# Batch 0 in two passes over half the weights, with the weight conversion spread over 24 units

## The chip, the cores and the metric

The kernel runs on one core of a Trainium2 chip. The core has five engines with queues of their own: TensorE (PE, its weight loads shown apart as PEld), VectorE (DVE), ScalarE (ACT), GpSimd (POOL) and SyncE (SP), which here only issues DMAs. The metric is the device time of one execution in microseconds (us); the time of a kernel is the median over runs. A profile is one execution more, with every instruction's start and end; its span is the time from the first to the last instruction, and its own device time is a little longer than the span.

## What is computed

The input x has 8 batches of 3008 positions by 256 channels. The reference takes the real part of a two-dimensional Fourier transform of each batch and sends every position through a two-layer network with a soft threshold between the layers:

```
X = np.fft.fft(np.fft.fft(x, axis=1), axis=2).real
h = X @ w_in
g = np.where(h >= 1, h, np.where(h <= -1, 0.0, (h + 1) ** 2 / 4))
out = g @ w_out
```

w_in is 256 by 2048 and w_out 2048 by 256. Both come as 64-bit floats, of which the kernel sees the two 32-bit halves.

## The kernel before

**Units.** A batch is cut into 3 chunks (one of 482 columns, two of 512; each column stands for a position and its mirror image, the two signs `sg`), and the 2048 hidden channels into 16 tiles `f` of 128. One chunk with one `f` is a unit; 8 x 3 x 16 = 384 units in all, taken chunk by chunk, `f` from 0 to 15 in each. `gemm1(i)` (from L343) makes the hidden values of unit i: six matmuls into two PSUM banks of the tag `uv` (three banks), then on DVE `us` (L356) and the two halves of `h` (L358, L359), then on ACT the soft threshold's square `a` (L362, L363), then on DVE the minimum and maximum that join them (`g`, L368 or L372). `gemm2(i)` (from L385) multiplies with w_out and adds into four PSUM banks, one for each half of the output channels and each sign. It runs four units behind `gemm1` (`LAG`), and at the last `f` of a chunk the four sums are copied out (L413 to L417) and sent to DRAM.

**Precision.** PE multiplies in a fast format after a value is split into a high and a low part, three products for each one. In the first 16 units (`NATIVE`) `gemm2` multiplies plain 32-bit floats instead, one slower product each, so that w_out need not be split yet and `g` need not be split at all. From unit 16 on, `gh` (ACT, L375) and `gl` (POOL, L377) are the parts of `g`.

**Weights.** Sixteen jobs of 512 KB convert the weights, eight for each matrix, in the order in, in, out, out for each quarter of the hidden channels. A job's steps have letters: `l` the load (SP), `a` two integer operations on DVE (L185, L186), `b` three ACT operations (L191 to L193), `c` two DVE operations (L198, L199), and the multiplication L212, called `d` where POOL does it and `v` where DVE does. A quarter of w_in is then folded with two small matrices on PE, because the real transform over the channels is moved into the weights (`f`, L231 and L232; two folds for a quarter), and split (`s`, L246). Row 0 of the second fold is brought into a column `delta` by four DMAs issued by ACT (L238). `o` splits an eighth of w_out (L152, L153).

**Transforms.** The Fourier transform of a batch is eight pieces of stage 1 (an addition `y`, matmuls L260, copies `z`), one small piece `nyquist`, whose row goes through DRAM and comes back spread over all partitions (`nyb`), and six pieces of stage 2 (matmuls L320, split into `pqh` and `pql`). For batch 0 the pieces stand in the start's hand-written list `START` and in `STEPS`; for a batch b+1 they lie between the units of batch b.

**Order.** `START` and `STEPS` are lists of such steps. Up to unit 15 (`PINNED`) every engine runs in exactly the order of the program text. Later the framework's scheduler orders by priority. In a unit the steps ahead of the bar `|` run between `a` and `g`, those behind it after `g`. A buffer tag has a few slots; a tile takes a slot when one is free, and a slot is free when all that reads its last tile is done. The tags that matter: `h` and `a` (three slots each, shared by the units' tiles and by the jobs' working tiles, even jobs in `h`, odd ones in `a`), `gh` and `gl` (four), `xt` (four input tiles), `o` (two output tiles).

Of the kernel before, what the change touches and what calls it, by code (L numbers as in the profile page):

```python
# [100 lines left out]
def fft_ffn_kernel(ctx: ExitStack, tc: tile.TileContext, x, cst, w_in, w_out, out):  # L101
# [114 lines left out]
    def split_w_out(q):  # L216
# [5 lines left out]
        split(*(wo[t][:, fs].rearrange("p f e -> p (f e)") for t in ("woh", "wol")), wo32[q // 2][:, q % 2])  # L222

    folds = {}

    def fold_w_in(n):
# [6 lines left out]
        if m == 1:  # L233
            row = sb.tile([1, CH], F32, tag="us", name=f"row_{f4}", bufs=2)
            nc.scalar.activation(row, pt[0:1], AF.Copy)
# [322 lines left out]
```

## Time and profile before

| what | us |
|---|---|
| median of 3 runs (lowest, highest) | 1791.31 (1790.23, 1791.47) |
| the profiled execution, device time | 1789.41 |
| its span | 1787.5 |
| PE busy | 1748.2 |
| DVE busy | 1430.2 |
| ACT busy | 1343.0 |
| POOL busy | 1186.5 |

The share of busy time of PE is 98%, so what can be won lies where PE is not busy or runs at a lowered clock. The page's second part shows these places as slices of the span; each of the 40 slices is 44.7 us long.

### The profile page before, as it was taken

The page shows a single profiled execution, that of the slowest core. Times are in us where ns is not written, and L with a number is a line of the kernel's source. Part 1 is how long each engine was busy: PE and PEld are TensorE (multiplying, and loading weights), DVE is VectorE, ACT ScalarE, POOL GpSimd, SP SyncE. Part 2 cuts the span into 40 slices and gives each one's busy share as a digit, 9 for nine tenths or more (in the row PEclk, how much of TensorE's full clock was granted, in tenths as well). Part 3 has the DMA queues.
Part 4 walks back from the last instruction along what each step waited for, and adds up shares of the span by engine and source line. Part 5 has one row for each costly group of instructions (what it writes and reads, how often), then busy time and mean ns, then how long its engine had stood idle before and what let it go on. Part 6 is the DMA issues. An engine that isn't in the chain of part 4 may idle for free.

```text
span 1787.5 us, 21542 instructions
## 1 busy us (share of the span) xinstructions
PE 1748.2 (98%) x7822; PEld 1408.4 (79%) x7822; DVE 1430.2 (80%) x1733; ACT 1343.0 (75%) x1571; POOL 1186.5 (66%) x829
## 2 busy tenths in 40 slices
PE   7789999999999999999999999999999999999998
PEld 5346888888888788887888888888888888887876
DVE  4887788878887888778878788787888788888886
ACT  4666787787777877778777777778777787777775
POOL 1233876777768766777667876677776766767776
PEclk7799999999999999999999999999999999999999
DMA  8111110110010100101001100011000000000000
GB/s 249 36 53 49 45 51 10 50 50 27 24 42 27 49 18 24 51 27 53 30 1 51 49 30 30 9 51 49 27 24 33 1 23 30 13 24 5 18 24 24
DMA packets 30026, 66.33 MB, mean 37 GB/s; under 512 B 5088, under 2 KB 9312, under 8 KB 29920
## 3 DMA queue, kind: packets, MB, share of 16 engines
q1 hardware_dynamic: 27580, 64.95, 11.2%
q8 instruction: 61, 1.00, 0.2%
q14 instruction: 45, 0.37, 0.1%
q10 hardware_dynamic: 2340, 0.02, 0.1%
HBM read 40.22 MB, written 24.72 MB: 36 GB/s over the span
## 4 chain that ended last, share of the span: by engine, by line
PE 43%; ACT 18%; POOL 16%; DVE 11%; issue 11%; DMA 1%; ACTq 0%; POOLq 0%; SPq 0%; DVEq 0%
PE acc L408 26%; POOL gl L377 15%; PE uv L353 13%; DVE h L372 7%; ACT a L363 6%; ACT gh L375 5%; ACT a L362 4%; PE s L320 2%; PE s L260 1%; ACT z L276 1%; DVE h L358 1%; DVE h L359 1%; POOL y L122 1%; DVE g L368 1%; DVE cv L186 1%
## 5 line engine op out<-in xcount | busy, mean ns | idle before, releaser
L377 POOL TENSOR_TENSOR gl<-h,gh 128x512 fp32r<-128x512 f32 (+1 forms) x736 | 1057.2, 1459 | 448.5 <-ACT gh L375 425.2
L372 DVE SCALAR_TENSOR_TENSOR h<-a,h 128x1024 f32<-128x1024 f32 (+1 forms) x368 | 560.6, 1524 | 236.4 <-ACT a L363 234.8
L375 ACT ACTIVATE gh<-h 128x1024 fp32r<-128x1024 f32 (+1 forms) x368 | 384.6, 1045 | 352.4 <-DVE h L372 338.4
L408 PE MATMUL acc<-gh,woh 128*128 128x512 f32 (+1 forms) x1472 | 586.7, 399 | 3.2 <-DVE o L417 2.2
L408 PE MATMUL acc<-gl,woh 128*128 128x512 f32 (+1 forms) x1472 | 575.3, 391 | 1.0 <-POOL gl L377 0.9
L408 PE MATMUL acc<-gh,wol 128*128 128x512 f32 (+1 forms) x1472 | 575.0, 391 | 0.0
L362 ACT ACTIVATE a<-h,biases 128x1024 f32<-128x1024 f32 (+1 forms) x384 | 431.4, 1124 | 31.3 <-DVE h L359 29.5
L363 ACT ACTIVATE a<-a 128x1024 f32<-128x1024 f32 (+1 forms) x384 | 398.7, 1039 | 7.6
L408 PEld LDWEIGHTS acc<-gh,woh 128*128 128x128 f32 x1472 | 277.7, 189 | 63.9 <-DVE o L417 5.7
L408 PEld LDWEIGHTS acc<-gl,woh 128*128 128x128 f32 x1472 | 277.6, 189 | 62.6 <-POOL gl L377 2.3
L353 PE MATMUL uv<-pqh,wh 128*128 128x512 f32 (+1 forms) x768 | 310.5, 404 | 14.8 <-DVE us L356 8.8
L408 PEld LDWEIGHTS acc<-gh,wol 128*128 128x128 f32 x1472 | 277.3, 188 | 54.4
L358 DVE TENSOR_TENSOR h<-us,uv 128x512 f32<-128x512 f32 (+1 forms) x384 | 259.7, 676 | 67.2 <-POOL gl L377 21.3
L353 PE MATMUL uv<-pql,wh 128*128 128x512 f32 (+1 forms) x768 | 301.6, 393 | 0.0
L353 PE MATMUL uv<-pqh,wl 128*128 128x512 f32 (+1 forms) x768 | 301.3, 392 | 0.0
L356 DVE SCALAR_TENSOR_TENSOR us<-nyb,delta,uv 128x512 f32<-128x512 f32 (+1 forms) x384 | 278.4, 725 | 7.0 <-PE uv L353 6.9
L359 DVE TENSOR_TENSOR h<-us,uv 128x512 f32<-128x512 f32 (+1 forms) x384 | 256.1, 667 | 0.0
L353 PEld LDWEIGHTS uv<-pqh,wh 128*128 128x128 f32 x768 | 145.5, 189 | 60.7 <-DVE us L356 14.6
L353 PEld LDWEIGHTS uv<-pqh,wl 128*128 128x128 f32 x768 | 145.6, 190 | 31.9 <-issue 3.7
L353 PEld LDWEIGHTS uv<-pql,wh 128*128 128x128 f32 x768 | 145.3, 189 | 29.7 <-DVE pql L153 0.2
L122 POOL TENSOR_TENSOR y<-x 96x512 f32<-96x512 f32 x58 | 104.9, 1808 | 31.2 <-PE s L260 16.5
L276 ACT ACTIVATE z<-s 64x192 f32<-64x192 f32 x246 | 83.2, 338 | 21.0 <-PE s L263 9.1
(56 smaller groups left out, 662.1 us busy)
## 6 DMA issues: line engine op xcount, KB each, us to landing
x<-in_x_dram SPq DMA_DIRECT2D x64, 384.0 KB, 3.5
out_dram<-o SPq DMA_DIRECT2D x30, 512.0 KB, 2.8
out_dram<-o SPq DMA_DIRECT2D x16, 482.0 KB, 2.9
nyb<-nyr SPq DMA_DIRECT2D x24, 256.0 KB, 3.3
raw<-in_moe_w_in_dram SPq DMA_DIRECT2D x4, 512.0 KB, 5.4
raw<-in_moe_w_out_dram SPq DMA_DIRECT2D x4, 512.0 KB, 10.6
raw_woh<-in_moe_w_out_dram SPq DMA_DIRECT2D x2, 512.0 KB
raw_woh<-in_moe_w_in_dram SPq DMA_DIRECT2D x2, 512.0 KB, 3.5
```

Source lines behind the costliest of these rows:

```text
L122: (engine or nc.gpsimd).tensor_tensor(y, t[:, 0], t[:, 1], op=ALU.add)
L276: nc.scalar.activation(dst, src, AF.Copy)
L353: nc.tensor.matmul(t[:, :n], w[m][:, cols], r[:, m, :n], start=(j == 0), stop=(j == 2))
L356: nc.vector.scalar_tensor_tensor(us, nyb[b, k][:, :n], delta[:, f : f + 1], uv[0], op0=ALU.mult, op1=ALU.add)
L358: nc.vector.tensor_tensor(h[:, 0], us, uv[1], op=ALU.subtract)
L359: nc.vector.tensor_tensor(h[:, 1], us, uv[1], op=ALU.add)
L362: nc.scalar.activation(a, h, AF.Relu, bias=half, scale=0.5)
L363: nc.scalar.activation(a, a, AF.Square)
L372: nc.vector.scalar_tensor_tensor(h, a, 1.0, h, op0=ALU.min, op1=ALU.max)
L375: nc.scalar.activation(gh, h, AF.Copy)
L377: nc.gpsimd.tensor_tensor(gl[:, sg], h[:, sg], gh[:, sg].bitcast(F32), op=ALU.subtract)
L408: nc.tensor.matmul(acc[:, :n], w, g[:, sg], start=(f == 0 and j == 0), stop=(last and j == len(terms) - 1))
```

## The change

1. **Two passes over batch 0.** The list `units` replaces the division of i by 16. In batch 0 the three chunks are first taken with `f` 0 to 7 (units 0 to 23), then with `f` 8 to 15 (units 24 to 47). At the end of a chunk's first pass its four sums go through `o` tiles to a DRAM tile; two units before the end of its second pass they are loaded again, and the copy at the end becomes an addition on DVE for all four.
2. **14 jobs over 24 units.** Because the second half of the weights is first used in unit 24, `STEPS` now reaches from unit 0 to 23: a full job in each of units 0 to 3, about half a job in each later one. `EARLY_BANKS` goes from 18 to 13, `PINNED` from 16 to 18, and the pieces of batch 1 start at unit 18 (`NEXT`) instead of 16.
3. **`d` becomes `v`.** All 14 multiplications L212 of these jobs move from POOL to DVE. Their buffers change: the last two of w_out stay in the job's working tile.
4. **g one unit later.** Up to unit 18, `activate(i - 1)` runs after the `h` of unit i.
5. **delta by matmuls.** Four matmuls of one row each and one ACT copy replace four DMAs issued by ACT.
6. **The start.** All additions `y` on DVE, two of them ahead of the first fold, the loads l4 and l5 ahead of the rest, the `nyquist` piece's copies ahead of the others, nine warm-up matmuls instead of seven and in one bank.
7. **Smaller moves.** The folding matrices use a slot of `nyb`; for later batches `nyquist_spread` is issued at the start of each pair of stage 2 pieces instead of three at once.

```diff
 START = (
-    "l0 k l1 m0 x0 x1 x2 x3 x4 x5 x6 x7 "
-    "a0 b0 a1 b1 c0 v0 y0 p0 z0 p8 c1 v1 y1 p1 z1 Y2 f0 y3 s0 p2 z2 Y4 f1 y5 s1 p3 p4 w3 y6 w4 p5 w5 y7 p6 w6 p7 w7 "
-    "l4 n0 l5 l2 l3 l8 l9 l6 l7 l12 l13 n1 l10 l11 n2 l14 l15 p9 q9 p10 q10 a4 b4"
+    "l0 k l1 m0 x0 x1 x2 x3 x4 x5 x6 x7 l4 l5 "
+    "a0 b0 a1 b1 c0 v0 y0 p0 t0 z0 c1 y1 v1 p1 p8 z1 n0 l2 l3 l6 l7 n1 l8 l9 l10 l11 n2 l12 l13 l14 l15 "
+    "y2 y3 f0 p2 z2 p3 s0 y4 w3 f1 y5 p4 p5 y6 s1 w4 e0 p6 w5 y7 p7 w6 w7 p9 p10 q9 q10 a4 b4"
 )
 STEPS = {
-    0: "c4 d4 a5 b5 |",
-    1: "c5 d5 a2 b2 |",
-    2: "f2 f3 c2 d2 a3 b3 | s2 s3",
-    3: "p11 c3 d3 a8 b8 | q11",
...
-    17: "o7 |",
+    0: "c4 v4 a5 b5",
+    1: "c5 v5 a2 b2",
+    2: "f2 f3 c2 v2 a3 b3 s2 s3",
+    3: "e1 c3 v3 a6 b6",
+    4: "c6 v6 p11 q11",
+    5: "a7 b7",
+    6: "c7 v7 p12 q12",
+    7: "a8 b8",
+    8: "c8 v8",
+    9: "a9 b9",
+    10: "c9 v9 a10 b10",
+    11: "f4 f5 s4 s5",
+    12: "e2 c10 v10 p13 q13",
+    13: "a11 b11",
+    14: "c11 v11 p14 q14",
+    15: "o0 o1 a12 b12",
+    16: "c12 v12 o2",
+    17: "o3 a13 b13",
+    18: "c13 v13 o4",
+    19: "o5 a14 b14",
+    20: "f6 f7 s6 s7",
+    21: "e3 c14 v14 a15 b15",
+    22: "o6 c15 v15",
+    23: "o7",
 }
-RAW = {0: "gh", 1: "gh", 4: "gh", 5: "gh", 2: "woh", 3: "woh", 8: "woh", 9: "woh"}
-RAW |= {6: "wol", 7: "wol", 12: "wol", 13: "wol", 10: "xt", 11: "xt", 14: "xt", 15: "xt"}
+RAW = {0: "gh", 1: "gh", 4: "gh", 5: "gh", 2: "woh", 3: "woh", 6: "woh", 7: "woh"}
+RAW |= {8: "wol", 9: "wol", 10: "wol", 11: "wol", 12: "xt", 13: "xt", 14: "xt", 15: "xt"}
...
+    def spread_delta(f4):
+        row = deltas.pop(f4)
+        pt = fft_bank(0, f"delta_{f4}")
+        for i in range(4):
+            nc.tensor.matmul(pt[:, i : i + 1], row[:, i * P : (i + 1) * P], one[0:1], start=True, stop=True)
+        nc.scalar.activation(delta[:, f4 * 4 : f4 * 4 + 4], pt[:, :4], AF.Copy)
...
-            with nc.allow_non_contiguous_dma(reason="one row of w_in to a column"):
-                for i in range(4):
-                    nc.scalar.dma_start(
-                        delta[:, f4 * 4 + i : f4 * 4 + i + 1], row[:, i * P : (i + 1) * P].rearrange("o (p x) -> o p x", x=1)
-                    )
+            deltas[f4] = row
...
+    units = [(0, k, f) for v in range(2) for k in range(NCHUNK) for f in range(v * NFT // 2, (v + 1) * NFT // 2)]
+    units += [(b, k, f) for b in range(1, NB) for k in range(NCHUNK) for f in range(NFT)]
...
+    def load_parts(k):
+        for dh in range(2):
+            o = outs[k, dh] = sb.tile([P, 2, CH], F32, tag="o", name=f"os_{k}_{dh}", bufs=2)
+            nc.sync.dma_start(o[:, :, : WIDTH[k]], parts.pop((k, dh))[:, :, : WIDTH[k]])
...
+                        if add:
+                            nc.vector.tensor_tensor(o[:, sg, :n], acc[:, :n], o[:, sg, :n], op=ALU.add)
+                        elif sg:
...
+            if half_way:
+                parts[k, dh] = dr.tile([P, 2, CH], F32, tag="part", name=f"part_{k}_{dh}", bufs=6)
+                nc.sync.dma_start(parts[k, dh][:, :, :n], o[:, :, :n])
...
-            gemm1(i, STEPS.get(i, ""))
+            gemm1(i)
+            if b == 0 and r > per // 2 and r % (NFT // 2) == NFT // 2 - 2:
+                load_parts(units[i][1])
+            if i <= PINNED and i:
+                activate(i - 1)
+            if i >= PINNED:
+                activate(i)
+            run_steps(STEPS.get(i, ""))
```

More of the change, by code (lines that the diff above doesn't have):

```diff
@@ L136, in fft_ffn_kernel @@
     delta = wts.tile([P, NFT], F32, name="delta")
-    biases = wts.tile([P, 3], F32, name="biases")
-    for i, v in enumerate((0.5, 1151.0, 255.0 * 2**23)):
+    biases = wts.tile([P, 4], F32, name="biases")
+    for i, v in enumerate((0.5, 1151.0, 255.0 * 2**23, 1.0)):
         nc.vector.memset(biases[:, i : i + 1], v)
-    half, above, top = (biases[:, i : i + 1] for i in range(3))
+    half, above, top, one = (biases[:, i : i + 1] for i in range(4))
     early = [0]
@@ L221, in split_w_out @@
         fs = slice(q * m, (q + 1) * m)
-        split(*(wo[t][:, fs].rearrange("p f e -> p (f e)") for t in ("woh", "wol")), wo32[q // 2][:, q % 2])
-    folds = {}
+        split(*(wo[t][:, fs].rearrange("p f e -> p (f e)") for t in ("woh", "wol")), wo32[q])
+    folds, deltas = {}, {}
+    def spread_delta(f4):
[4 more added lines that the diff above has]
+        nc.scalar.activation(delta[:, f4 * 4 : f4 * 4 + 4], pt[:, :4], AF.Copy)
     def fold_w_in(n):
@@ L264, in stage1_sums, with stage1_last @@
         s1[b, q] = bank
+    def stage1_last(b, bank):
+        pd = bank[:NA, GPC * 96 : GPC * 96 + 2 * NC]
+        for m in range(2):
+            nc.scalar.activation(zt[b][m * NA : (m + 1) * NA, :, P], pd[:, m * NC : (m + 1) * NC], AF.Copy)
     def stage1_copy(b, q, vector=False):
         z, bank = zt[b], s1.pop((b, q))
+        if q == 0 and b:
+            stage1_last(b, bank)
         pt = bank[:, : GPC * 96].rearrange("p (i n) -> p i n", i=GPC)
@@ L312, in stage2_sums @@
         if h % 2 == 0:
+            if b:
+                nyquist_spread(b, k)
             pq[b, k] = tuple(
@@ L339, in fft_pieces, with gemm1 @@
         return pieces
-    acts = {}
-    def gemm1(i, steps):
-        bk, f = divmod(i, NFT)
-        b, k = divmod(bk, NCHUNK)
+    units = [(0, k, f) for v in range(2) for k in range(NCHUNK) for f in range(v * NFT // 2, (v + 1) * NFT // 2)]
+    units += [(b, k, f) for b in range(1, NB) for k in range(NCHUNK) for f in range(NFT)]
+    n_units = len(units)
+    per = NCHUNK * NFT
+    fronts, acts = {}, {}
+    def gemm1(i):
+        b, k, f = units[i]
         n = WIDTH[k]
@@ L363, in gemm1, with activate @@
         nc.scalar.activation(a, a, AF.Square)
-        before, after = steps.split("|") if steps else ("", "")
-        run_steps(before)
+        fronts[i] = h, a
+    def activate(i):
+        n = WIDTH[units[i][1]]
+        h, a = fronts.pop(i)
         if i < NATIVE:
@@ L369, in gemm1 @@
             acts[i] = (g,)
-            run_steps(after)
             return
@@ L408, in gemm2 @@
                     nc.tensor.matmul(
-                        acc[:, :n], w, g[:, sg], start=(f == 0 and j == 0), stop=(last and j == len(terms) - 1)
+                        acc[:, :n], w, g[:, sg], start=(begin and j == 0), stop=(last and j == len(terms) - 1)
                     )
@@ L424, in fft_ffn_kernel @@
     nc.gpsimd.memset(warm, 0.0)
-    for _ in range(7):
-        nc.tensor.matmul(fft_bank(0, "warm"), warm[:, :P], warm, start=True, stop=True)
+    warm_bank = fft_bank(0, "warm")
+    for _ in range(9):
+        nc.tensor.matmul(warm_bank, warm[:, :P], warm, start=True, stop=True)
     n1 = XC
```

67 lines of the change are left out of this document (25 added, 42 removed).

## The prediction

> **What bounds the kernel now.** First the busy time in four stretches (columns: stretch, its length, then busy us and count for PE, PEld, DVE, ACT, POOL, then PE's granted clock, the DMA share, GB/s).
>
> ```profile
> 39.70:63.00 23.30, 17.59 (x41) 10.30 (x41) 22.20 (x33) 14.84 (x20) 5.07 (x5) 0.65 0.41 141
> 63.00:150.00 87.00, 74.30 (x214) 40.60 (x213) 72.79 (x101) 53.42 (x72) 22.00 (x19) 0.91 0.12 32
> 150.00:188.30 38.30, 38.30 (x159) 27.25 (x158) 30.64 (x38) 30.23 (x44) 21.70 (x16) 1.00 0.19 59
> 188.30:1787.50 1599.20, 1590.17 (x7307) 1311.43 (x7305) 1289.46 (x1531) 1228.49 (x1400) 1132.64 (x780) 1.00 0.09 30
> ```
>
> After 150 us PE is full, so only the first 150 us can get shorter, or the rest get worse. Between 40 and 63 us DVE is busy 22.2 of 23.3, with PE at 0.65 of its clock. Next, PE's prices, from the chain that ended last (start, length, what).
>
> ```profile
> 140.00 4.68 PE acc L408 x8
> 144.68 1.31 PE uv L353 x6
> 145.99 3.23 PE acc L408 x8
> ...
> 169.94 1.40 PE uv L353 x6
> 171.33 0.87 PE s L260 x8
> 172.20 2.82 PE acc L408 x12
> ...
> 188.49 1.39 PE uv L353 x6
> ```
>
> A gemm1 costs 1.31 at 482 columns and 1.39 at 512; a gemm2 of plain floats 3.23 at 482, so 3.43 at 512; a split one 2.82; a transform piece about 0.9. At 172.20 stands the first split product, gemm2 of unit 16, behind gemm1 of unit 20; four gemm1 on, **gemm1 of unit 24 starts at 188.49**. That is my marker: the changed kernel has by then laid out all weights too, and from there both have the same full PE. Now DVE's prices between 40 and 150 us (groups by shape: count, busy us, mean ns, idle before), and one group, L358, from 300 to 1700 us.
>
> ```profile
> L368 DVE SCALAR_TENSOR_TENSOR g<-a,h 128x964 f32<-128x964 f32 x15 | 17.7, 1180 | 4.4 <-issue 2.6 <-ACT row L235 1.1 <-ACT a L363 0.7
> ...
> L356 DVE SCALAR_TENSOR_TENSOR us<-nyb,delta,uv 128x482 f32<-128x482 f32 x15 | 10.6, 707 | 0.3 <-PE uv L353 0.3
> ...
> L186 DVE TENSOR_SCALAR cv<-raw_woh 128x512 uint32<-128x512 uint32 x4 | 6.1, 1513 | 0.0
> ```
> ```profile
> L358 DVE TENSOR_TENSOR h<-us,uv 128x512 f32<-128x512 f32 (+1 forms) x319 | 215.6, 676 | 55.2 <-POOL gl L377 18.7 <-DVE us L356 1.0 <-PE uv L353 0.5
> ```
>
> A unit needs 0.71 + 2 x 0.68 + 1.18 = 3.2, and about 3.0 at 482 columns, as neighbours on DVE overlap by 0.08 (at 68.35 below, 0.69 ends past 68.96); 3.2 at 512. With a whole job on top DVE is the bound: PE needs only 1.31 + 3.23 = 4.5 a unit. L186 is the odd one:
>
> ```profile
> 40.62 0.42 DVE L186 TENSOR_SCALAR cv<-raw 128x512 uint32<-128x512 uint32 x1
> 45.03 1.38 POOL L212 TENSOR_TENSOR cv<-cv 128x512 f32<-128x512 f32 x1 [18.75 <-DVE cv L199]
> 127.64 1.29 POOL L122 TENSOR_TENSOR y<-x 96x512 f32<-96x512 f32 x1 [1.49 <-DMA x<-in_x_dram]
> 128.04 1.44 DVE L198 SCALAR_TENSOR_TENSOR cv<-raw,cv 128x512 f32<-128x512 uint32 x1
> ```
>
> Alone it takes 0.42; where POOL's multiplication L212 runs beside it, 1.5 (the group's mean; in each unit with a job POOL starts one like that of 45.03). DVE waits for POOL there; at 128.04 L198 takes 1.44 instead of 0.69, beside one of POOL's additions.
>
> **The change, part by part. The start.** Rows of the timeline:
>
> ```profile
> 11.44 0.31 SPq L115 DMA_DIRECT2D x<-in_x_dram  x1
> 13.50 0.69 DVE L212 TENSOR_TENSOR cv<-cv 128x512 f32<-128x512 f32 x1
> 21.51 1.91 PE L231 MATMUL wps<-cv,cm 128*128 128x512 f32 x4
> 24.55 2.62 ACTq L238 DMA_DIRECT2D delta<-row  x4
> 27.22 2.09 ACT L276 ACTIVATE z<-s 64x192 f32<-64x192 f32 x6 [2.70 <-issue]
> 35.27 3.75 PE L320 MATMUL s<-cs,z 128*128 128x128 f32 x16 [1.63 <-DVE z L274]
> 41.32 0.72 DVE L356 SCALAR_TENSOR_TENSOR us<-nyb,delta,uv 128x482 f32<-128x482 f32 x1 [0.27 <-PE uv L353]
> 68.35 0.69 DVE L153 TENSOR_TENSOR pql<-s,pqh 128x512 fp32r<-128x512 f32 x1 [0.96 <-ACT pqh L152]
> 68.96 0.71 DVE L356 SCALAR_TENSOR_TENSOR us<-nyb,delta,uv 128x482 f32<-128x482 f32 x1
> ```
>
> Four delta DMAs hold ACT for 2.6 us just ahead of the copies that stage 2 (35.27) waits for. They go; in their place four tiny matmuls, which the trace doesn't show, cost PE between nothing and 1.7, twice the stage 1 piece of eight records (0.87 at the full clock); I take 0.9, that piece. The input additions go earlier and the first fold no longer stands ahead of two of them, for which I take another 2.3. Stage 2 then starts 4.9 sooner, at 30.4, and `us` of unit 0 at 36.4 instead of 41.3. Ends: 2.6 (only the DMAs) and 8.7, where the last input sets it: its load is issued at 11.44, and the start's loads take 11 us to land (11.2 by the next row), so about 22.7 plus an addition, a piece and its copies.
>
> ```profile
> DMA to landing us min/median/max: 10.9/11.2/12.3
> ```
>
> **Units 0 to 3.** Before, `us` of unit 4 starts at 68.96, 27.6 behind that of unit 0. Four L186 fall from 1.51 to 0.42: -4.4. Four multiplications come from POOL: 4 x 0.69 = +2.8. The first g leaves unit 0: -1.1. The stage 2 split at 68.35 moves to unit 4 with its wait of 0.96: -1.6. New is a wait: g late means `h` of unit 1 still holds its slot when unit 2 asks for one; the other two hold jobs 4 and 2. Job 4's is freed by folds f2 and f3 on PE, and `us` of unit 2 is queued ahead on DVE. At the clock of 0.65 a fold takes 1.91 / 0.65 = 2.9; f3 can't start before `us` of unit 2, so `h` waits about 3.0, and behind it on DVE g, c2, v2, a3. Sum 26.3; `us` of unit 4 at 62.7.
>
> That clock is a choice. With the clock restored the wait is 2.0 and all is 1 us earlier. The row for it:
>
> ```profile
> 136.72 0.77 PE L353 MATMUL uv<-pqh,wh 128*128 128x482 f32 x1 [3.60 <-DVE us L356]
> ```
>
> After this gap of 3.60 the next gemm2 takes 4.68 (at 140.00 above), the one behind it 3.23. The Trainium skill, "TensorE: Matmul & The Clock Gate", What's actually happening, has PE fall to half its clock after an idle window of about 3.4 us and rise again after one of busy work. That speaks against this part of the change, which leaves PE 1.3 us of work in units of 5; the trace agrees (4.68). By the rule the folds would run at half clock, f3 would take 3.8, and the sum would be 1 us later than mine.
>
> **Units 4 to 10** carry half a job each: c and v 1.8 (three operations of 0.69, less the overlaps), or a 0.7 (twice 0.42), and unit 4 and 6 a split of 0.6. DVE: 5.4 + 3.7 + 5.4 + 3.7 at 482 columns, 5.0 + 3.9 + 5.7 at 512: 32.8. PE has as much (4.5 to 5.6 a unit) but is a unit ahead when unit 4 begins. So `us` of unit 11 is at 95.5.
>
> **Unit 11** has f4 and f5, and the `h` ring is short again (jobs 8 and 10, `h` of unit 10): DVE waits for f5. Fold end 97.9 to 98; then h, g, two splits 3.5 in the shadow of gemm2 of unit 7 (3.2), and two sums' copies; `us` of unit 12 at 102.7, PE at about 102.5.
>
> **Units 12 to 23.** PE per unit 1.39 + 3.43 = 4.8 up to gemm2 of unit 15, then 1.39 + 2.82 = 4.2; pieces p13, p14, three of batch 1 and two delta spreads 0.9 each, f6 and f7 3.4 (1.91 each, less 0.2 of overlap): 63.7. DVE needs 4 to 5.5 a unit up to 17, under PE. So gemm1 of unit 24 could start at 102.5 + 63.7 = 166.2.
>
> Here I add **8 us of stalls**, between 0 and 18, for the split units 16 to 23. Their rows, from the page:
>
> ```profile
> L377 POOL TENSOR_TENSOR gl<-h,gh 128x512 fp32r<-128x512 f32 (+1 forms) x736 | 1057.2, 1459 | 448.5 <-ACT gh L375 425.2
> L372 DVE SCALAR_TENSOR_TENSOR h<-a,h 128x1024 f32<-128x1024 f32 (+1 forms) x368 | 560.6, 1524 | 236.4 <-ACT a L363 234.8
> L375 ACT ACTIVATE gh<-h 128x1024 fp32r<-128x1024 f32 (+1 forms) x368 | 384.6, 1045 | 352.4 <-DVE h L372 338.4
> L362 ACT ACTIVATE a<-h,biases 128x1024 f32<-128x1024 f32 (+1 forms) x384 | 431.4, 1124 | 31.3 <-DVE h L359 29.5
> L363 ACT ACTIVATE a<-a 128x1024 f32<-128x1024 f32 (+1 forms) x384 | 398.7, 1039 | 7.6
> ```
>
> A split unit holds its `h` slot for 1.3 + 1.12 + 1.04 + 1.52 + 1.05 + 2 x 1.46 = 9 us, and even with three slots `h` waits for POOL here and there (18.7 in all in the L358 row). Job 12 keeps one from unit 15 to 20, job 14 one from 19 to 22. With two slots the pitch is 4.5 at best, near PE's 4.8; with one, 9. Also POOL must fold inputs whose `xt` slots jobs 13 to 15 still hold, and DVE's c and v beside POOL's `gl` take up to 1.44 instead of 0.69, as at 128.04. ACT has b, o and gh at once. Four units of lag hide part of it; 8 is nearer the three-slot row than the one-slot figure.
>
> **Afterwards.** Three more chunk ends, and three at which DVE adds four sums. Before, PE waited 2.2 in all for these copies at 24 ends:
>
> ```profile
> L408 PE MATMUL acc<-gh,woh 128*128 128x512 f32 (+1 forms) x1472 | 586.7, 399 | 3.2 <-DVE o L417 2.2
> ```
>
> That is 0.1 an end. Bounds 0 and 8 (four additions of 0.69, three times, with nothing hidden); I take 1.5. The round trip through DRAM and the loads two units ahead lie beside PE work; the late `nyb` loads have tens of us to spare.
>
> **The sum.** Marker 166.2 + 8 = 174.2 instead of 188.5: 14.3. At the marker the new kernel has done eight units more at 512 columns, 8 x (0.08 + 0.20) = 2.2, and one transform piece less, 0.9: +1.3. Less 1.5: 14.1 gained, span 1773.4, device time of such an execution 1775.3 (1789.41 - 14.1). The median of the runs shown, 1791.31, is 1.9 above the profiled time; from it I get **1777**.
>
> **The rivals.** (1) **The ring and POOL swallow it**: stalls of 18 in units 16 to 23 and only 2.6 from the start leave about 2: 1789. For it: the 18.7 above; against: only 16 to 22 are short of slots. (2) **Slower, by the `h` ring alone**: if units 17 to 23 go through one slot, each takes 9 + 1.3 instead of 5.2, +36 over the 166.2: marker 202, time 1791 + 202 - 188.5 + 0.2 = 1805. It decides from a pitch of gemm1 of 5.2 + 22 / 7 = 8.3 us in these units; below that it is a gain. Against it: folds f6 and f7 free job 12's slot at unit 20, and the order is no longer fixed there. (3) **The start isn't shorter** and four chunk ends cost their 8: 1777 + 4.9 + 6.5 = 1788. (4) **No stalls**, and the start bound by its loads: 1777 - 8 - 3.8 = 1765.
>
> **How the numbers follow.** A measurement of this kernel can tell 0.2%, 3.6 us, so faster means below 1787.7. Forecast with stalls up to about 14, faster throughout: 0.70. Rival 4, faster: 0.08. Rival 1: 0.07 and rival 3: 0.06, both at the boundary, so a third of them, 0.04, counts as faster and 0.09 as the same. Rival 2: 0.09, and 0.01 of it at a pitch near 8.3, where it is the same. That would be 0.82, 0.10 and 0.08; with 0.02 moved from faster for what I haven't seen, faster 0.80, same 0.11, slower 0.09. The range is 1766 to 1790: rival 4 at its near edge, rival 1 at the other.
>
> **What would show it.** Right: L186 at 0.42 up to unit 15; ACT without DMA issues; stage 2 of batch 0 near 30; the first `us` near 36 and the fifth near 63; `h` waiting for PE's folds in units 2 and 11; PE full from about unit 12; the first split gemm2 near 155 instead of 172.2. Wrong: `h` waiting long for POOL's `gl` in units 17 to 22, gemm1 of unit 24 later than 185, gaps of PE at the chunk ends of batch 0, or stage 2 still at 35.

## The result and the profile after

| | before | after |
|---|---|---|
| median of the runs on the same chip (lowest, highest) | 1790.77 (1787.38, 1791.47) | 1778.62 (1778.06, 1779.30) |
| ratio after to before (95% interval) | | 0.9936 (0.9919 to 0.9953) |
| the profiled execution, device time | 1789.41 | 1778.06 |
| its span | 1787.5 | 1776.3 |

The change makes the kernel 0.64% faster, 12.2 us by the medians and 11.2 us by the two spans. I had forecast 14.1 us; the time of 1777.0 with its range of 1766 to 1790 holds. Several terms behind it were off in both directions and cancel in part, and the largest single loss of the changed kernel behind its start is one that I had priced at 0.9 us.

First the busy time of the changed kernel in stretches that answer to those of before (stretch, length, busy us and count of PE, PEld, DVE, ACT, POOL, PE's granted clock, DMA share, GB/s).

```profile
35.00:63.00 28.00, 20.45 (x58) 12.10 (x57) 26.19 (x44) 21.31 (x29) 0.98 (x2) 0.82 0.27 102
63.00:150.00 87.00, 80.98 (x258) 46.41 (x257) 72.07 (x105) 52.38 (x69) 10.36 (x9) 0.96 0.08 25
150.00:188.30 38.30, 33.27 (x146) 24.56 (x145) 36.27 (x42) 30.46 (x46) 23.65 (x19) 1.00 0.36 111
188.30:1776.30 1588.00, 1580.02 (x7276) 1304.51 (x7275) 1285.63 (x1536) 1223.24 (x1394) 1127.13 (x776) 1.00 0.10 34
```

From 63 to 150 us PE is now busy 81.0 of 87 instead of 74.3. In the third row the picture is the other way round: before, PE was full there (38.30 of 38.30), now it is busy 33.27 and DVE 36.27. That is where a part of the gain went.

The next rows, of the timeline of the changed kernel, are the marks of the start and of the units up to 11 (start, length, what, and in brackets the idle time before it and what ended it).

```profile
28.59 3.75 PE L336 MATMUL s<-cs,z 128*128 128x128 f32 x16 [1.63 <-DVE z L295]
34.35 0.72 DVE L376 SCALAR_TENSOR_TENSOR us<-nyb,delta,uv 128x482 f32<-128x482 f32 x1
43.87 0.42 DVE L192 TENSOR_SCALAR cv<-raw_woh 128x512 uint32<-128x512 uint32 x1
46.47 0.66 DVE L378 TENSOR_TENSOR h<-us,uv 128x482 f32<-128x482 f32 x1 [1.22 <-PE wps L249]
58.11 0.71 DVE L376 SCALAR_TENSOR_TENSOR us<-nyb,delta,uv 128x482 f32<-128x482 f32 x1
93.07 0.74 DVE L376 SCALAR_TENSOR_TENSOR us<-nyb,delta,uv 128x512 f32<-128x512 f32 x1
95.18 0.69 DVE L378 TENSOR_TENSOR h<-us,uv 128x512 f32<-128x512 f32 x1 [1.36 <-PE wps L249]
```

Stage 2 starts at 28.59, where it was 35.27; `us` of unit 0 stands at 34.35 and that of unit 4 at 58.11. `h` waits for the folds in units 2 and 11, as forecast, but 1.22 and 1.36 us only. Up to here the changed kernel is ahead of the forecast, by 2.4 us at unit 11 (93.07 for 95.5).

Then comes unit 12, here with PE, ACT and DVE of the same timeline in order of time.

```profile
100.89 1.05 PE L240 MATMUL delta<-biases,row 1*128 1x1 f32 x8
...
104.10 1.15 ACT L382 ACTIVATE a<-h,biases 128x1024 f32<-128x1024 f32 x1 [3.03 <-DVE h L379]
105.28 1.06 ACT L383 ACTIVATE a<-a 128x1024 f32<-128x1024 f32 x1
106.24 0.15 ACT L241 ACTIVATE delta<-delta 128x4 f32<-128x4 f32 x1
106.45 2.08 PE L336 MATMUL s<-cs,z 128*128 128x128 f32 x8 [4.51 <-ACT delta L241]
108.32 4.95 PE L432 MATMUL acc<-g,wo 128*128 128x512 f32 x8
114.01 0.75 DVE L376 SCALAR_TENSOR_TENSOR us<-nyb,delta,uv 128x512 f32<-128x512 f32 x1 [4.12 <-PE uv L373]
```

The delta spread's matmuls are done at 101.94. The bank that they wrote is the one into which the next transform piece (L336) must write, and it comes free when ACT has copied 128 x 4 values out of it. That copy takes 0.15 us, but it stands in ACT's queue behind both operations of `a` of unit 12, and these wait for that unit's `h`. So PE stands still for 4.51 us, and what follows runs at a lowered clock (granted 0.50 from 104.21 to 111.03 us): the piece takes 2.08 instead of 1.05, the gemm2 behind it 4.95 instead of 3.6 (3.59 at 114.51 us). `us` of unit 13 comes 12.07 us after that of unit 12 (101.94). The same spread in unit 3, at 52.88, hurt nothing: the next transform piece came only at 57.16, without a gap.

The last part is PE's idle time in units 16 to 23, all of its gaps between 126 and 205 us.

```profile
142.02 1.13 PE L274 MATMUL s<-cs,y 96*128 96x96 f32 x8 [1.45 <-POOL y L129]
153.81 0.50 PE L373 MATMUL uv<-pqh,wh 128*128 128x512 f32 x1 [1.18 <-DVE us L376]
162.81 0.50 PE L373 MATMUL uv<-pqh,wh 128*128 128x512 f32 x1 [1.15 <-DVE h L379]
180.11 0.49 PE L373 MATMUL uv<-pqh,wh 128*128 128x482 f32 x1 [1.95 <-DVE us L376]
184.75 0.48 PE L373 MATMUL uv<-pqh,wh 128*128 128x482 f32 x1 [0.45 <-DVE h L379]
185.98 0.48 PE L373 MATMUL uv<-pqh,wh 128*128 128x482 f32 x1 [0.30 <-DVE us L376]
```

They sum to 6.5 us, and by the table below PE loses about 9.4 there; the rest is in smaller pieces and not in the clock, which is granted at 1.00 from 126 to 205 us. The first is POOL's addition for batch 1, and the five others are DVE, late with `us` or `h`. PE runs ahead of DVE here: the last three stand in gemm1 of units 24 and 25. All 2304 matmuls of gemm1 are in the trace, six a unit, so the 145th is the start of gemm1 of unit 24, the marker of the prediction. It starts without a gap:

```profile
176.92 0.38 PE L373 MATMUL uv<-pqh,wh 128*128 128x482 f32 x1
```

The rows behind both causes, of SP's, POOL's and DVE's timelines:

```profile
135.61 0.72 DVE L206 SCALAR_TENSOR_TENSOR cv<-raw,cv 128x512 uint32<-128x512 uint32 x1
136.36 16.52 SPq L122 DMA_DIRECT2D x<-in_x_dram  x5
139.87 2.10 POOL L129 TENSOR_TENSOR y<-x 96x512 f32<-96x512 f32 x1 [37.94 <-PE uv L373]
...
144.94 1.48 DVE L192 TENSOR_SCALAR cv<-raw 128x512 uint32<-128x512 uint32 x1
158.61 1.48 DVE L192 TENSOR_SCALAR cv<-raw 128x512 uint32<-128x512 uint32 x1 [1.86 <-POOL gl L399]
171.45 3.07 DVE L192 TENSOR_SCALAR cv<-raw 128x512 uint32<-128x512 uint32 x1
181.18 2.32 DVE L394 SCALAR_TENSOR_TENSOR h<-a,h 128x1024 f32<-128x1024 f32 x1
```

Job 12's c step ends at 136.33; 0.03 us later SP issues the first load of batch 1's input, into the `xt` slot that job 12 held, and 3.5 us later POOL adds. DVE pays in three coins: the operation that took 0.42 at 43.87 takes 1.48 and 3.07 beside POOL, the joining operation L394 takes 2.32 instead of 1.21, and at 158.61 the a step of job 14 waits for a slot of the `h` ring that a `gl` still reads.

To add up what PE loses I take, for each point in time, that time less the sum of all matmuls until then, each at its form's full-clock pitch (the lower quartile of the distance to the next record in both traces). What is left is idle time and lowered clock:

| PE's lost us up to | 41 | 63 | 100 | 112 | 140 | 200 | 1750 | all matmuls at full clock |
|---|---|---|---|---|---|---|---|---|
| before | 21.8 | 34.7 | 44.6 | 48.7 | 55.6 | 57.7 | 86.4 | 1694.3 |
| after | 16.0 | 26.5 | 26.7 | 33.9 | 33.8 | 43.2 | 70.1 | 1700.0 |

16.3 us less are lost. 5.7 us of work are new, 3.6 of it the delta spreads and 1.7 the two more warm-up matmuls. The difference, 10.6, agrees with the spans within 0.6. Of the changed kernel's loss after 100 us, 7.2 fall to unit 12 (up to 112 us) and 9.4 to units 16 to 23 (140 to 200); between units 4 and 11 PE loses nothing (26.5 to 26.7).

### The profile page after: what moved, and what is told of

It is laid out like the page before. It is cut to its first block, busy times and chain, and to the rows that moved or that the text cites. A ratio compares the mean times of both kernels' runs of the same rounds, so it can differ in the third digit from the quotient of the medians.

```text
span 1776.3 us, 21601 instructions
## 1 busy us (share of the span) xinstructions
PE 1744.0 (98%) x7858; PEld 1407.5 (79%) x7858; DVE 1438.4 (81%) x1762; ACT 1344.3 (76%) x1575; POOL 1164.7 (66%) x813
## 4 chain that ended last, share of the span: by engine, by line
PE 67%; POOL 9%; ACT 8%; DVE 8%; issue 6%; DMA 1%; POOLq 0%; ACTq 0%; SPq 0%; DVEq 0%
PE acc L432 42%; PE uv L373 21%; POOL gl L399 9%; DVE h L394 4%; ACT a L383 3%; ACT gh L397 3%; PE s L336 2%; ACT a L382 2%; PE s L274 2%; DVE h L378 1%; DMA x<-in_x_dram 1%; DVE h L379 1%; POOL y L129 1%; ACT z L297 0%; DVE us L376 0%
## 5 line engine op out<-in xcount | busy, mean ns | idle before, releaser
L394 DVE SCALAR_TENSOR_TENSOR h<-a,h 128x1024 f32<-128x1024 f32 (+1 forms) x368 | 555.0, 1508 | 220.3 <-ACT a L383 218.7
L373 PE MATMUL uv<-pqh,wh 128*128 128x512 f32 (+1 forms) x768 | 308.7, 402 | 12.5 <-DVE us L376 5.7
```

The source lines that it names most:

```text
L373: nc.tensor.matmul(t[:, :n], w[m][:, cols], r[:, m, :n], start=(j == 0), stop=(j == 2))
L394: nc.vector.scalar_tensor_tensor(h, a, 1.0, h, op0=ALU.min, op1=ALU.max)
```

## Experiments

Each kernel was timed beside the kernel before, whose median stood at 1790.3 to 1790.8 on these chips. "A" and "B" are the theories in the expectations. The `us` times are from the timeline of DVE.

**e1: the second delta spread one unit later.** Is unit 12 a matter of the shared bank, and what is it worth at the end?

```diff
-    12: "e2 c10 v10 p13 q13",
-    13: "a11 b11",
+    12: "c10 v10 p13 q13",
+    13: "e2 a11 b11",
```

> The changed kernel with one step moved: the delta spread of the third quarter (e2) from unit 12, ahead of the transform piece p13, to unit 13. Theory A: in the changed kernel PE stands 4.5 us in front of p13 (L336, 106.45 us) because p13 shares its only PSUM bank with e2, whose copy on ACT is queued behind a and its square of unit 12; the clock then falls and gemm2 of unit 8 takes about 1.5 us more, p13 1. With e2 in unit 13 no such gap is left, us of unit 13 starts 6 to 7 us sooner than 114.0, and as PE is the bound the end comes 4 to 7 us sooner: 1772 to 1775. Rival B: from unit 18 on DVE is the bound (36.3 of 38.3 us busy between 150 and 188), so units 18 to 23 take the gain back: us of unit 24 and the end move by under 2 us, 1777 to 1779.

Measured: 1776.33 us (ratio to before 0.9915, 0.9901 to 0.9929). The timeline of e1, the same place:

```profile
101.14 1.05 PE L336 MATMUL s<-cs,z 128*128 128x128 f32 x8
102.03 3.60 PE L432 MATMUL acc<-g,wo 128*128 128x512 f32 x8
...
108.13 1.05 PE L240 MATMUL delta<-biases,row 1*128 1x1 f32 x8 [1.10 <-DVE pql L160]
109.10 3.70 PE L432 MATMUL acc<-g,wo 128*128 128x512 f32 x8
```

The gap of 4.51 is gone and the clock stays up: 1.05 and 3.60 for 2.08 and 4.95, and `us` of unit 13 at 107.99, 6.0 sooner. So the cause is shown; a gap of 1.10 is left ahead of the moved spread. But the 6.0 shrink to 5.3 at unit 16, 4.1 at unit 19, 3.4 at unit 24 and 2.6 at the end of the span: more than half is gone by the end, 1.9 of it in units 16 to 23. There e1 has the changed kernel's wait for batch 1's first addition (1.41 us, before 136.67) and behind it a granted clock of 0.50 from 138.63 to 142.05, which the changed kernel hasn't. The time lies between A and B. The intervals of the two ratios overlap; the gain of 2.3 in the medians rests on the trace as well.

**e2: the multiplications back on POOL** (`v` in all 14 places to `d`, nothing else).

```diff
-    0: "c4 v4 a5 b5",
-    1: "c5 v5 a2 b2",
+    0: "c4 d4 a5 b5",
+    1: "c5 d5 a2 b2",
...
```

> The changed kernel with the 14 weight multiplications back on POOL, all else as changed. Theory A: each L193 (the second integer operation) beside them goes from 0.42 to 1.5 us, the multiplication itself (0.69) leaves DVE: 14 x (1.09 - 0.61) = 6.7 us more of DVE, and as DVE is the bound in units 0 to 3 and 18 to 23, some 3 to 6 us of it reach the end: 1782 to 1785. Rival B: DVE has room where PE is the bound, so nothing or under 2 us reaches the end; us of unit 4 then starts 1 to 2 us later than 58.1 and the rest is caught up by unit 12.

Measured: 1786.36 us (0.9979, 0.9968 to 0.9991), 7.7 above the changed kernel and above the range of A. Timeline of e2, DVE and POOL in unit 1 and 2:

```profile
38.66 1.50 DVE L193 TENSOR_SCALAR cv<-raw 128x512 uint32<-128x512 uint32 x1
44.46 1.38 POOL L222 TENSOR_TENSOR cv<-cv 128x512 f32<-128x512 f32 x1 [4.59 <-DVE cv L206]
49.79 0.66 DVE L378 TENSOR_TENSOR h<-us,uv 128x482 f32<-128x482 f32 x1 [3.03 <-PE wps L249]
```

The stretch comes back, but on the second integer operation (L193, 1.5 for 0.42), since L192 now starts just ahead of POOL. DVE gains 0.69 a job and loses 1.1. In unit 2 the folds wait for POOL, and `h` waits 3.03 us instead of 1.22. `us` of unit 4 is 4.0 later (0.8 of it already at unit 0, which the edit doesn't touch), that of unit 24 6.5.

**e3: g in its own unit again** (up to unit 17 the steps, then the activation, as in the old order).

```diff
-            if i <= PINNED and i:
-                activate(i - 1)
-            if i >= PINNED:
-                activate(i)
-            run_steps(STEPS.get(i, ""))
+            if i < PINNED:
+                run_steps(STEPS.get(i, ""))
+            activate(i)
+            if i >= PINNED:
+                run_steps(STEPS.get(i, ""))
```

> The changed kernel with g in its own unit, behind the unit's steps, up to unit 17 (as in the kernel before), all else as changed. Theory A: g one unit later is worth little or costs: h of unit 1 and unit 10 then free their slots in time, so the waits for the folds in units 2 and 11 (1.2 and 1.4 us in the changed kernel) go, while with half a job in the unit DVE now waits for a and its square where the steps are short: 2.1 us of ACT less the steps' 0.7 to 1.8, up to 1.5 in 14 units, of which PE being the bound hides most. The end moves by under 2 us, 1777 to 1780. Rival B: the order h, steps, g puts DVE's wait on the path in the units with a short step: 5 us or more later, 1784 or above.

Measured: 1792.97 us (1.0015, 1.0005 to 1.0024). Undoing this one step takes the whole gain away, as B had it and more. The timeline of e3 in units without a long step on DVE:

```profile
69.51 1.01 ACT L383 ACTIVATE a<-a 128x964 f32<-128x964 f32 x1
70.56 1.17 DVE L391 SCALAR_TENSOR_TENSOR g<-a,h 128x964 f32<-128x964 f32 x1 [1.54 <-ACT a L383]
71.63 0.71 DVE L376 SCALAR_TENSOR_TENSOR us<-nyb,delta,uv 128x482 f32<-128x482 f32 x1
```

`us`, `h`, both operations of `a` and `g` stand in one chain: from `us` at 66.31 to the next at 71.63 it takes 5.3 us, whatever DVE has to do. With half a job a unit DVE has less than that, so it waits for ACT. Units 8, 9 and 13 take 5.6 us each here and 5.05, 4.2 and 4.8 in the changed kernel. By the start of gemm1 of unit 12 PE has lost 8.7 us more than in the changed kernel, by that of unit 24 12.5: the light units are the largest part of the cost, not all of it. My prediction had counted this part only for what it moves out of unit 0 and for the wait that it adds in unit 2, not for the wait that it takes away in every light unit.

**e4: the old kernel with only the new start.** `START`, the warm-ups, `EARLY_BANKS` and the first delta by matmuls from the changed kernel; all else as before.

```diff
-    "a0 b0 a1 b1 c0 v0 y0 p0 z0 p8 c1 v1 y1 p1 z1 Y2 f0 y3 s0 p2 z2 Y4 f1 y5 s1 p3 p4 w3 y6 w4 p5 w5 y7 p6 w6 p7 w7 "
...
+    "a0 b0 a1 b1 c0 v0 y0 p0 t0 z0 c1 y1 v1 p1 p8 z1 n0 l2 l3 l8 l9 n1 l6 l7 l12 l13 n2 l10 l11 l14 l15 "
+    "y2 y3 f0 p2 z2 p3 s0 y4 w3 f1 y5 p4 p5 y6 s1 w4 e0 p6 w5 y7 p7 w6 w7 p9 p10 q9 q10 a4 b4"
```

> The kernel before with the start of the changed one alone (order of steps, additions on DVE, first delta column by matmuls, warm-up in one bank); the 16 units and their steps are as before. Theory A: the start's gain is carried whole, because the units after it are bound by DVE whatever their first instant: us of unit 0 starts 5 to 7 us sooner than 41.3, and the end comes 5 to 7 us sooner than that of the kernel before: about half of what the whole change brings. Rival B: the weights' loads, now later in the queue, hold up units 1 to 3, and less than 3 us is left at the end.

Measured: 1786.53 us (0.9973, 0.9962 to 0.9983), 4.3 faster. `us` of unit 0 is at 36.05 (41.32 before), 5.3 sooner, with the second weight load landed at 8.92 us by the DMA records, close to the 8.77 of before. 5.0 of it are left at unit 4, 2.6 at unit 12 and 3.5 in the span. That lies between A and B: the start's gain is carried in part.

**e10: the first delta by four DMAs again**, the rest of the changed kernel as it is (`EARLY_BANKS` goes to 12, as one bank fewer is asked for).

```diff
-... s1 w4 e0 p6 ...
+... s1 w4 p6 ...
             deltas[f4] = row
+            if f4 == 0:
+                for i in range(4):
+                    nc.scalar.dma_start(
+                        delta[:, i : i + 1], row[:, i * P : (i + 1) * P].rearrange("o (p x) -> o p x", x=1)
+                    )
```

> The changed kernel with the first delta column by four DMAs of ACT again, the later three by matmuls. Theory A: ACT is held 2.6 us between the fold's row and the copies of stage 1, which then end 2 to 2.6 us later; us of unit 0 starts near 36.5 instead of 34.3, and 1.5 to 2.5 us reach the end: 1780 to 1781. Rival B: the copies have that room, because the additions now come earlier, and under 1 us reaches the end.

Measured: 1783.30 us (0.9963, 0.9950 to 0.9977), 4.7 above the changed kernel. Timeline of e10, ACT and PE:

```profile
21.36 2.52 ACTq L258 DMA_DIRECT2D delta<-row  x4
...
30.60 3.36 PE L342 MATMUL s<-cs,z 128*128 128x128 f32 x16 [1.63 <-DVE z L301]
```

Four issues hold ACT for 2.52 us and stage 2 comes 2.0 later (28.59). That is the size I had given to this step. At the end it is more than that, above A: 4.8 in the span. Counted as in the table of lost time, PE has lost 2.3 more by the start of gemm1 of unit 48 and 3.4 more behind it, and 0.9 of work is gone. Behind unit 48 this kernel does what the changed one does; why it loses more there stays open.

**e9: one pass.** The old kernel with the new start, `v` for `d` and g one unit later, but with one pass, 16 jobs over the old units, and the later deltas by DMA.

```diff
 before, with the start of e4, and:
-    0: "c4 d4 a5 b5 |",
+    0: "c4 v4 a5 b5",
...
+            if i <= PINNED and i:
+                activate(i - 1)
+            if i >= PINNED:
+                activate(i)
+            run_steps(STEPS.get(i, ""))
```

> All of the change but the two passes: batch 0 taken once, chunk by chunk, the 14 jobs over 16 units as in the kernel before (a full job in each), with the new start, the multiplications on DVE, and g one unit later; the delta columns of the later quarters by DMA. Theory A: DVE has 5.3 to 5.5 us of work in a unit with a full job (2.9 for the unit, 2.5 for the job), PE 4.5, so each of the first 16 units costs 0.8 to 1 us more than PE needs, and the folds' waits come four units apart: us of unit 15 near 132 to 136 instead of 124.6, and the end 6 to 11 us later than the changed kernel, 1784 to 1789; the two passes are then worth about half of the whole. Rival B: the passes are worth little, since what they save up to unit 15 comes back in units 18 to 23, where the spread jobs meet POOL's gl: the end is within 3 us of the changed kernel, 1776 to 1782.

Measured: 1782.05 us (0.9952, 0.9939 to 0.9966), at the edge of B. The two passes, with the later deltas by matmuls, are worth 3.4 of the 12 us. The way there is instructive: at unit 15 the changed kernel is 17.4 us ahead by `us` (124.58, in e9 141.96), at unit 24 it is 2.1 behind (185.22 and 183.15). `us` is DVE's, though, and DVE isn't what bounds the rest. PE starts gemm1 of unit 24 at 176.92, in e9 at 180.51: 3.6 ahead, and the spans say 3.9. PE has lost 14.0 less than in e9 by the start of gemm1 of unit 12, and 7.8 less by that of unit 24. So spreading the jobs buys 14 us of PE's time and the units up to 23 take almost half of it back; there jobs and split products lie on top of each other, where e9 has its jobs out of the way by unit 16. That this is the cause is tested next.

**What holds units 16 to 23.** Two suspects: the slots (the jobs' working tiles in the `h` and `a` rings), and the split products themselves, for which POOL, DVE and ACT are needed beside the jobs. All of the next six kernels contain e1's edit.

*e5* takes the tiles of jobs 12 and 14 out of the ring, into slots of `pqh` and `pql` that are free then; *e8* takes those of jobs 4, 8, 12 and 14.

```diff
-        t = sb.tile([P, 2, CH], U32, tag="ha"[n % 2], name=f"cv_{n}", bufs=3)
+        tag = {4: "pqh", 8: "pqh", 12: "pqh", 14: "pql"}.get(n, "ha"[n % 2])
+        t = sb.tile([P, 2, CH], U32, tag=tag, name=f"cv_{n}", bufs=3 if len(tag) == 1 else 4)
```

(e5 has only 12 and 14 in that table.)

> The kernel with the delta spread moved (1776.3), and the working tiles of jobs 12 and 14 in the free fourth slots of pqh and pql instead of slots of h. In that kernel units 18 to 23 take 46.4 us from us to us, where PE has 33 us of work. Theory A: the h ring is the cause (us of unit 18 starts at 135.4, its h only 7 us later, when gl of unit 16 is done and two operations of job 13 that the order puts there). With three slots for the units again the six units take 37 to 41 us and the end comes 4 to 8 us sooner: 1768 to 1772. Rival B: DVE is simply full there, as its operations beside POOL's take 1.2 to 3 us instead of 0.4 to 0.7; then the six units keep 44 us or more and the end moves by under 2 us.

> As the run with jobs 12 and 14 off the h ring, with jobs 4 and 8 in the slot of pqh too. Theory: h of units 2 and 11 no longer waits for the folds (1.2 and 1.4 us in the changed kernel), so us of unit 4 starts about 1 us sooner than 58.5 and that of unit 12 1 to 2 us sooner than 102.3. In unit 11 PE itself runs the folds and has gemm2 behind, so at the end at most 1 us more than in that run.

Measured: e5 1776.42 us (0.9925, 0.9912 to 0.9938), e8 1773.70 us (0.9907, 0.9894 to 0.9920). From `us` of unit 18 to that of unit 24 it takes 42.7 in e5 and 40.35 in e8, where e1 has 46.4 (135.41 to 181.80). The profiled executions of both began three us later than e1's (`us` of unit 0 at 37.52 and 37.59), so their ends tell little. In e8 the wait in unit 11 is gone too. Neither is the full recovery that the ring alone would have brought: e5 lies between its two theories in these units and has B's time. e8 is 2.7 below e5 where at most 1 was expected (their intervals overlap); what jobs 4 and 8 add beyond their own two waits isn't shown.

*e6* has gemm2 in plain floats up to unit 23 (`NATIVE = 24`): no split product until the jobs are done, for 5.2 us more of PE work.

> The kernel with the delta spread moved, and NATIVE 24 instead of 16: units 16 to 23 multiply plain floats too. That takes gh (ACT) and gl (POOL) out of these eight units, and puts 8 x 0.6 = 4.9 us of matmul more on PE. Theory B (POOL's gl stretches DVE and holds h): the six units 18 to 23 become bound by PE, 33.4 + 3.7 = 37 us instead of 46, us of unit 24 starts 7 to 10 us sooner, and the end 4 to 8 us sooner: 1768 to 1772. If gl has no part in it, the extra PE work is a plain loss: 1779 to 1782.

Measured: 1777.30 us (0.9925, 0.9913 to 0.9937). From unit 18 to 24 it takes 39.1, and `us` of unit 24 is 6.8 sooner than in e1. PE's gemm1 of unit 24 isn't: it starts at 173.74, in e1 at 173.52, with 2.4 less lost and 2.6 more work done. Neither theory's time came: the loss by the splits is real, and this remedy costs as much as the illness.

*e7* starts batch 1's pieces at unit 24 instead of 18 (`NEXT = 24`).

> The kernel with the delta spread moved, and NEXT 24 instead of 18: loads, additions and pieces of batch 1 begin at unit 24, when no job holds an input slot. Theory: four additions of POOL (1.3 to 2.3 us each), waits for the loads (3 to 4 us) and 4 pieces' copies of ACT leave units 18 to 23. If POOL's waits for the loads are what holds gl and so h, the six units fall from 46 to about 40 us; what returns later, as the pieces then lie denser, is hidden, as PE is the bound there, and the end comes 2 to 5 us sooner. If not, under 2 us either way.

Measured: 1782.79 us (0.9956, 0.9945 to 0.9968), 6.5 above e1: the pieces must then be done in fewer units, and what is saved up to unit 24 (`us` at 182.26, e1 181.80: nothing) is lost in units 24 to 35 (`us` of unit 32 at 221.80, e1 215.12). The expectation had under 2 us either way for this case; it missed that cost. Starting the pieces later is no remedy.

*e12* and *e11* make only units 16 to 19 plain (`NATIVE = 20`, 2.6 us more of PE work), e12 on top of e1, e11 on top of e8.

```diff
-NATIVE = NFT
+NATIVE = 20
```

> The kernel with four jobs off the h ring (1773.7), and NATIVE 20: four units more with plain floats. Theory: PE gets 4 x 0.6 = 2.5 us more to do, and gl and gh leave units 16 to 19, where the run before loses some 5 us of PE between 140 and 160; if half of the loss goes, both cancel: 1772 to 1775. If gl's neighbourhood is all of the loss there, 1770 to 1772.

> e1 (second delta spread in unit 13; 1776.3) with gemm2 of units 16 to 19 in plain floats, and every job's working tile in the units' rings as in the changed kernel. It separates what e11 (e8 with the same four plain units, 1766.7, 7.0 below e8) had together. If units 16 to 23 lose time because split products and jobs share DVE, POOL and ACT there, whatever tile the jobs sit in, the four plain units bring here what they brought over e8: 1768 to 1771, and us of unit 24 starts 34 to 38 us behind that of unit 18. If the slots that jobs 12 and 14 hold decide, so that fewer splits only help with the jobs off the ring, as plain floats up to unit 24 brought nothing over e1 (1777.3), the time stays at 1774 to 1778.

Measured: e12 1774.54 us (0.9908, 0.9891 to 0.9926), in the range of its second theory; **e11 1766.66 us (0.9867, 0.9853 to 0.9880)**, below both of its theories, the fastest of all kernels here and 12.0 below the changed one. The busy time between 130 and 190 us (columns as above), first e1, then e12, e8 and e11:

```profile
130.00:190.00 60.00, 53.33 (x216) 36.65 (x215) 54.27 (x63) 44.26 (x64) 35.68 (x27) 0.97 0.29 90
```
```profile
130.00:190.00 60.00, 58.01 (x213) 36.36 (x212) 52.39 (x68) 42.93 (x64) 26.31 (x21) 0.97 0.31 90
```
```profile
130.00:190.00 60.00, 56.89 (x236) 41.03 (x235) 52.93 (x62) 47.65 (x69) 38.96 (x29) 0.97 0.26 77
```
```profile
130.00:190.00 60.00, 59.98 (x237) 39.85 (x237) 52.78 (x68) 44.79 (x68) 31.50 (x23) 1.00 0.29 86
```

PE is busy 53.3, 58.0, 56.9 and 60.0 of 60: only with both edits is it full and its clock at 1.00. The four plain units bring 1.8 us over e1, with overlapping intervals, and 7.0 over e8. Between the starts of gemm1 of units 12 and 24 PE loses 9.5 us in e1, 6.4 in e8, 6.8 in e12 and 2.1 in e11: both suspects are real, and there the two remedies about add up. By the table of lost time, e11 loses 9.6 less than e8 for 2.6 more of work: 6.8 of it between 100 and 200 us, 1.3 later, and 1.5 up to 100 us, where the two kernels do the same; that part is chance of the profiled executions.

Part of what the two edits do together isn't the slots. In e1 and e12, as in the changed kernel, batch 1's first input is loaded when job 12's c step ends, and PE waits for the addition. Timelines of e12, SP, POOL and PE:

```profile
132.43 11.21 SPq L122 DMA_DIRECT2D x<-in_x_dram  x3
136.15 1.89 POOL L129 TENSOR_TENSOR y<-x 96x512 f32<-96x512 f32 x1 [32.48 <-DMA x<-in_x_dram]
138.10 1.13 PE L274 MATMUL s<-cs,y 96*128 96x96 f32 x8 [1.42 <-POOL y L129]
139.40 4.54 PE L432 MATMUL acc<-g,wo 128*128 128x512 f32 x6
```

With job 12's tile out of the ring its steps come two units sooner in the order of DVE's queue, and so do the `xt` slot and the load. Timelines of e11:

```profile
116.70 23.73 SPq L122 DMA_DIRECT2D x<-in_x_dram  x6
120.21 3.59 POOL L129 TENSOR_TENSOR y<-x 96x512 f32<-96x512 f32 x1 [20.30 <-DMA x<-in_x_dram]
131.39 1.03 PE L275 MATMUL s<-cs,y 96*128 96x96 f32 x8
```

The load is issued at 116.70 instead of 132.43 and the addition done at 123.80; the piece follows at 131.39 without a wait, and between 126 and 205 us PE has no gap at all. So e8 and e11 test a bundle: free slots and earlier inputs. No run parts them. In the traces, e12 loses 5.5 more than e11 between 100 and 200 us, and 3.7 of that lie from 134 to 146, where this wait stands with a granted clock of 0.50 behind it (140.19 to 143.60).

## Why the prediction was right, and where it was off

By its own steps, forecast and measured:

| step | forecast | measured |
|---|---|---|
| `us` of unit 0 | 36.4 | 34.35 |
| units 0 to 3 | 26.3 | 23.76 |
| units 4 to 10 | 32.8 | 34.96 |
| unit 11 (`us` to `us`) | 7.2 | 8.87 |
| `us` of unit 12 | 102.7 | 101.94 |
| delta spread in unit 12 | 0.9 | 0.9 of work and 7.2 lost |
| stalls of units 16 to 23, up to gemm1 of unit 24 | 8 | 5.7 |
| gemm1 of unit 24 | 174.2 | 176.92 |
| lost behind it, against before | +1.5 | +1.3 |
| gain in the span | 14.1 | 11.2 |

- **The start: right in mechanism, its size within the scatter.** The four DMAs held ACT for 2.5 us and putting them back costs 2.0 there (e10). In this profile the new order of additions brought more than the 2.3 I took, but it is the soonest of ten: in the profiles of this kernel and of those here with the same start, `us` of unit 0 stands between 34.35 and 37.59, and the forecast of 36.4 lies inside.
- **Units 0 to 3: right in mechanism, the wait too dear.** L192 is at 0.42, `h` waits for the fold, but 1.22 us and not 3.0. I had taken f3 at the lowered clock of 0.65; the granted clock of 35 to 63 us came out at 0.82, and f3, the four records from 45.31, took 1.98. The Trainium skill's rule ("TensorE: Matmul & The Clock Gate", What's actually happening), weighed there, would have made it 3.8. Here PE's longest idle time ahead of the folds, 2.31 us before 39.68, is shorter than the 3.4 us of that rule, and yet the granted clock behind it is 0.50, from 39.35 to 42.77: two records of f2 took 1.94 there, the next two, at 44.01, 1.13. By f3 it was back. So I had the lowered clock right and its place wrong.
- **Why DVE's operations shrink.** I had put L186's 1.5 down to POOL's multiplication, and e2 agrees, though there it is the other integer operation that is stretched. But e2 and e3 show what I had not priced: with the multiplication on POOL the folds come later, and with g in its own unit the chain over ACT sets the pitch. g one unit later, which I had counted at -1.1 and a wait, is worth 14.4 here (e3).
- **Units 4 to 10**: 2.2 us slower than the sum of DVE's operations. PE has no gap and a full clock there (lost time 26.5 at 63 us, 26.7 at 100): it had caught up, and PE set the pitch, not DVE, as I had it.
- **Unit 12: this step failed.** I priced the spread by its matmuls and not by what its result blocks. The bank it writes is the one every transform piece needs, and its copy is last in ACT's queue. The step reads "two delta spreads 0.9 each"; the first of them cost 7.2 more by the table of lost time, and e1, by moving it one unit, shows it. The other, in unit 21, showed no such gap.
- **Units 16 to 23: near in size, partly right in mechanism.** 5.7 for 8 up to the marker, and most of the rest of the 9.4 in the three gaps of gemm1 of units 24 and 25. I had named the ring, POOL's inputs behind jobs 13 to 15's `xt` slots, and DVE beside `gl`. All three are in the rows; the slot at fault was job 12's. The rivals that gave the ring alone 18 us or a pitch of 10 were wrong: over the six units from 18 the pitch is 7.4 (140.76 to 185.22), and taking four jobs off the ring brings 2.6 us over e1, with overlapping intervals. One of my signs failed with this: PE was not full from unit 12 on.
- **The marker held.** gemm1 of unit 24 came 2.7 later than forecast and the gain in the span is 2.9 smaller; both kernels have by then done the same gemm2, and the changed one a transform piece less, as I had it. `us` of the same unit would have misled, since DVE lags behind PE there: it stands at 185.22, and e6 and e9 above show how it moves without the end.
- **Afterwards: right in sum, by luck in its parts.** Counted to the end of the span, PE loses 36.7 us behind the marker, 35.4 before. Up to the start of gemm1 of unit 48 that is 3.5 more than before, most of it in the gaps from 180.11 to 185.98 and not at the chunk ends, which I had priced; behind unit 48 it is 2.1 less (31.5 for 33.6). The fourteen profiles of this case lie between 30.6 and 35.0 there, so the 2.1 can't be given to the spreading of `nyquist_spread`.

Up to the marker the terms close. PE is through with gemm1 of unit 12 at 100.9 instead of 102.5 (1.6 sooner), has 63.6 of work from there instead of 63.7 (0.1), and loses 12.5 instead of 8: 6.8 in unit 12 (7.2 in the table, which counts from 100 us) and 5.7 behind it. That is 2.8 later, and 2.7 is measured. The total came out near because a sooner start and smaller stalls made up for over half of what the mispriced spread lost.

The parts don't add up. Undone one at a time, they cost 14.4 (g late), 7.7 (`v`), 4.7 (first delta) and 3.4 (two passes, against e9); the sum is 30 for a gain of 12. So they depend on each other; how, pair by pair, wasn't tried. What is shown is that units 16 to 23 took a part of two gains made ahead of them, those of e1's edit and of the two passes.

## What to carry to other kernels

Price a small operation by what waits for its result and for its buffer, not by its length: follow the copy that frees the bank through its engine's queue. When work is spread out to fill idle time, look at what will be running where its tail now lies, since a later crowded stretch takes back what is gained ahead of it. Judge an edit by PE's lost time and its work apart, and put a marker on the engine that bounds the rest: here gemm1 on PE told the end, and `us` of the same unit on DVE pointed the other way in e6 and e9.

## What the runs showed of the hardware that wasn't expected

- **DVE beside POOL can be stretched far more than the 1.5 us of before.** The integer operation of 0.42 us took 3.07 at 171.45, beside a memset of POOL from 171.21 and two `gl` from 171.70 to 174.24; it ended 0.28 after them. In units 0 to 3 of e2 it was the second integer operation that took 1.5; the first, started just ahead of POOL, took 0.42. POOL is stretched as well: its addition took 3.59 at 120.21 in e11, beside three operations of DVE with two inputs each (120.25 to 122.67), and 1.27 elsewhere.

The Trainium skill, "SBUF — State Buffer", Who interferes with whom, says that a DVE operation in a two-port mode and a POOL operation exclude each other for a whole instruction, by order of issue. The rows agree: DVE's stretched operation is about as long as what POOL does beside it, 1.48 for one operation of POOL, 3.07 for two behind a memset that had started 0.24 ahead of it; and the one that started ahead of POOL, at 38.32 in e2 with POOL from 38.48, took 0.42. That the integer operation runs in such a mode no run here shows.

- **A gap can cost PE twice.** After 4.51 us of standing, PE needed 2.08 for the piece of 1.05 and 4.95 for the gemm2 of 3.60: 2.4 us on top. The gap of 1.42 in e12 was followed by a slower gemm2 too: six of its eight records took 4.54, where all eight take 3.6. The granted clock was 0.50 behind it, from 140.19 to 143.60. A gap of 1.41 in e1 did the same (138.63 to 142.05), while behind one of 1.45 in the changed kernel, before 142.02, it stayed at 1.00. The rule on the clock cited above speaks of idle windows of about 3.4 us; here gaps less than half as long lowered the clock, and the length of the gap alone didn't decide. What does stays open.
- **The first loads don't land at one time.** The second weight load landed between 6.9 and 9.1 us in the profiled executions of these kernels, but that alone doesn't set the start: e1, at 6.90, has `us` of unit 0 at 34.40, the changed kernel, at 7.58, at 34.35, and e5, at 8.38, at 37.52. Two single profiles can differ by three us up to 40 us without a change in the start.
